# A first round over the key chunks with seven groups of queries, emitted with known landing times

## The chip, the cores and the metric

The kernel runs on one core of a Trainium2 chip. The metric is the device time of one execution in microseconds (us), and the median of several runs is quoted. The profile is that of one execution of the same program. PE is TensorE (PEld its weight loads), ACT is ScalarE, DVE is VectorE, POOL is GpSimd and SP is SyncE, which here only issues transfers.

## The reference

The reference is an attention with spatially reduced keys, followed by a two-layer feed-forward block over its output. Cut to what matters:

```python
B, C, H, W = 4, 128, 384, 32                 # N = H * W = 12288 queries of each b
kv_pool = kv.reshape(B, H // 4, 4, W // 4, 4, C).mean(axis=(2, 4))
k = v = kv_pool.reshape(B, -1, C) @ w_sr     # 768 keys of each b
s = (q @ k.transpose(0, 2, 1)) / np.sqrt(C)
a = np.exp(s - s.max(-1, keepdims=True))
a /= a.sum(-1, keepdims=True) + 1e-09
x = (a @ v).reshape(B * N, C)                # 49152 x 128
h = x @ w_in                                 # 128 x 2048
out = (h * (1.0 / (1.0 + np.exp(-1.702 * h)))) @ w_out
```

## The kernel before

**Tiling.** The 49152 queries form 96 groups of G = 512 (`NG`). The 768 keys of one batch element form JC = 6 chunks of 128. A unit of attention work is a pair (group i, chunk jc): one 128x512 score matmul (line 347), an exponential of its tile on ACT (line 349), and later the sums with the values, four 128-query tiles per group (line 360, four matmuls for each pair). A unit of feed-forward work is a pair (group g, chunk fc) with FCH = 16: one 128x512 matmul with `w_in` (line 593), the gelu on ACT (line 595), and one 128x512 matmul with `w_out` (line 603).

**Fills and drains.** The program is emitted in one fixed order. `seq` lists fills: one fill makes one to three units' matmuls into PSUM, then has ACT pass over all of them with one instruction into the buffer `ag`. Fill p uses banks 0 to 2 or 3 to 5 by the parity of p, so it waits until ACT has finished fill p-2. Fills are narrow at first: `sizes` gives two of one unit and then a number of two units, and after those all have three (K = 3); the last eight feed-forward fills have two units. Between two fills, drains are emitted: the matmuls that use what ACT has written (line 360 or 603). The loop at the end of the kernel decides how many drains fit, with a clock of its own in the emitting code: `now` is TensorE's position in units of one 512-column matmul, `end[p]` is when it thinks ACT will finish fill p, and `COST`, `COPY` and `free` hold the matmul times, the DVE copies, and when each accumulator bank becomes free. This clock decides the order of the instructions only; on the chip they wait on semaphores.

**Start.** POOL's queue issues the first loads in the order written in lines 245 to 257. A query group arrives from 256 KB of float32, a key chunk from 1 MB, both cast to bfloat16 by the transfer. Chunk 0 comes separately, through SP and a cast on the engines. For a chunk, `pool_chunk` (line 139: 16 small matmuls, then a DVE copy `pTc` at line 142) makes pooled columns; `key_and_value` (lines 161 and 162, copies at 163 and 164) makes keys `kT` and values `v`. For a query group, `transpose_q` (line 233, copy at line 239) makes `qT`. `first` says ahead of which fill each of these jobs stands. `warm(n)` puts n matmuls on ones (line 291), whose result nothing uses. The table `chunks` first runs over six groups for each chunk as it arrives, and then over the rest group by group.

**Later query groups.** Groups from 12 on come from `q_bf` with transposing transfers on SP (`load_qT`, line 215). Each is led by a one-column DVE memset (line 214) emitted when `TURN` reaches it. Line 412 is the score matmul of a pair whose exponential is computed on DVE (`early_fill`), emitted singly among the drains.

**End.** The last group (95) is drained by `drain_last` (line 631): 64 matmuls of 128 columns, spread over the four accumulator banks 2, 5, 6 and 7. One of these is still held by group 94 and is used from the tenth of these matmuls on. Group 94's result leaves its bank with a DVE transpose (line 614) after its last `w_out` matmul. Four copies (line 639) and two stores (line 642) end the program.

Of the kernel before, what the change touches and what calls it, by code (L numbers as in the profile page):

```python
# [24 lines left out]
def kernel(  # L25
# [8 lines left out]
    JC = J // 128  # L34
# [5 lines left out]
    NG = B * N // G  # L40
    NS = NG // 4
    GB = NG // B
# [38 lines left out]
    free = {2: 0.0, 5: 0.0, 6: 0.0, 7: 0.0}  # L81
    turns = [7, 6, 5]
    last_acc = 7
# [11 lines left out]
    def next_acc():  # L95
        return min((m for m in turns if m not in closes), key=lambda m: (max(free[m], now), turns.index(m)))
# [10 lines left out]
    now = 0.0  # L107
# [3 lines left out]
    def x_tile(s):  # L111
        return x[:, s % XS * SG:(s % XS + 1) * SG]
# [13 lines left out]
    def load_chunk(b, jc):  # L126

        a, ch = divmod(jc, HC)
        t = x_tile(XS - 1 - jc)
        nc.gpsimd.dma_start(out=t, in_=kv_r[b, a, ch])  # L130
        kv_tiles[b, jc] = t.rearrange("p (wp w1 c) -> p w1 wp c", w1=r, c=C)
# [75 lines left out]
    def cast_q(s):  # L207
        sl = slice(s * SG, (s + 1) * SG)
        nc.gpsimd.dma_start(out=q_bf[sl, :].rearrange("(p i) c -> p (i c)", p=128),
                            in_=q_flat[sl, :].rearrange("(p i) c -> p (i c)", p=128))  # L210
# [7 lines left out]
    QS = 3  # L218
    qs = [x_tile(XS - 1 - JC - s) for s in range(QS)]

    def load_q(s, lo, hi):
        nc.gpsimd.dma_start(  # L222
            out=qs[s].rearrange("p (g e) -> p g e", g=4)[:, lo:hi, :],
            in_=q_flat[s * SG + lo * G:s * SG + hi * G, :].rearrange("(g p i) c -> p g (i c)", p=128, i=4))
# [22 lines left out]
    load_chunk(0, 1)  # L247
    load_q(0, 2, 4)
    load_q(1, 0, 2)
    for jc in range(2, JC):  # L250
        load_chunk(0, jc)
    load_q(1, 2, 4)
    for s in range(2, QS):
        load_q(s, 0, 2)
        load_q(s, 2, 4)
    cast_q(3)
    cast_q(4)

# [68 lines left out]
    early = range(NG // R, NG // R + EARLY)  # L327
    rolling = [(i, JC - 1) for i in [*range(38, NG // R, 6), *range(57, 90, 6)]]
# [315 lines left out]


    NA, NM = NG * JC, NG * FCH
    chunks, sizes = [], [1] * 2 + [2] * 28
    chunks += [(0, 0), (1, 0), (0, 1), (1, 1)]
    chunks += [(i, jc) for i in range(2, 6) for jc in range(2)]
    chunks += [(i, jc) for jc in range(2, JC) for i in range(6)]  # L650
    chunks += [(i, jc) for i in range(6, NG) for jc in range(JC) if i not in early and (i, jc) not in rolling]
    seq, todo = [], []
    todo_early = [("a", t, a) for t in range(NT) for a in range(2) if (t // TS * TS + TS - 1) // 4 in early]
    for n in range(R):
        part = [c for c in chunks if c[0] // (NG // R) == n]
        while part:
            m = sizes.pop(0) if sizes else K
            seq.append(("a", part[:m]))
            part = part[m:]
# [34 lines left out]
    def later(g):  # L694
        extras.append((transpose_q, g))

    def jobs(p):

        nonlocal now
        for f, *args in first.get(p, ()):  # L700
            if f in COST:
                now = max(now, free[next_acc()])
            f(*args)
            if f in COST:
                now += COST[f][0]
                free[last_acc] = copied(f)

    def prepare(p):

        nonlocal now  # L710
        kind, part = seq[p]
        for i, jc in part:
            if (kind, i) not in begun:
                begun.add((kind, i))
                (background if kind == "a" else background_moe)(i)
            while kind == "a" and ((key_and_value, i // GB, jc) in extras or (transpose_q, i) in extras):
                f, *args = extras.pop(0)
                now = max(now, free[next_acc()]) + COST[f][0]
                f(*args)
                free[last_acc] = copied(f)  # L720

    first = {
        0: [(pool_chunk, 0, 0), (transpose_q, 0), (warm, 1), (key_chunk, 0, 0), (transpose_q, 1)],
        1: [(value_chunk, 0, 0), (warm, 1)],
        2: [(pool_chunk, 0, 1), (warm, 2), (key_and_value, 0, 1), (warm, 1), (transpose_q, 2)],
        3: [(transpose_q, 3)],
        4: [(transpose_q, 4)],
        5: [(transpose_q, 5)],
        6: [(pool_chunk, 0, 2)],
        7: [(key_and_value, 0, 2)],  # L730
        9: [(pool_chunk, 0, 3)],
        10: [(key_and_value, 0, 3)],
        12: [(pool_chunk, 0, 4)],
        13: [(key_and_value, 0, 4)],
        15: [(pool_chunk, 0, 5)],
        16: [(key_and_value, 0, 5), (later, 6)],
        17: [(later, 7)],
        18: [(later, g) for g in range(8, 12)]}

# [2 lines left out]
    COST = {pool_chunk: (1.9, 2.6), key_chunk: (0.3, 2.4), value_chunk: (0.3, 2.4),  # L744
            transpose_q: (1.05, 4.2), early_fill: (1.0, 5.5), key_and_value: (0.55, 3.5),
            transpose_pooled: (0.9, 3.6), make_k: (0.8, 3.2), make_v: (0.8, 3.7)}
# [8 lines left out]
    def on_dve(cost):  # L755
        nonlocal dve
        dve = max(dve, now + 1.0) + cost


    def copied(f):  # L760
        if f not in COPY:
            return now + COST[f][1]
        on_dve(COPY[f])
        return max(now + COST[f][1], dve)

    def fill(p):
        nonlocal now
        if p >= len(seq):
            return
        kind, part = seq[p]  # L770
        prepare(p)
        if p == 4:
            turns.insert(0, 2)
        if p == narrow - 5:
            for m in (2, 5):
                turns.remove(m)
        if p == narrow:
            assert not any(m in closes for m in (2, 5))
            now = max(now, free.pop(2), free.pop(5))
        lo = K * (p % 2)  # L780
        (fill_attn if kind == "a" else fill_moe)(part, banks[:, lo:lo + len(part), :])
        if p >= 2:
            now = max(now, end[p - 2] + HANDOVER / 2)
        now += len(part)
        begin = max(now + HANDOVER / 2, end[p - 1] if p else 0.0)
        if p and kind != seq[p - 1][0]:
            begin += SWITCH
        end.append(begin + FIXED + CHUNK * len(part))

    for p in range(2):  # L790
        jobs(p)
        fill(p)
    jobs(2)
    for n in range(len(seq)):
        fill(n + 2)
        jobs(n + 3)
        while True:
            room = room_ahead()
            limit = end[-1] - K - HANDOVER if n + 3 < len(seq) else 1e9
            bank = free[next_acc()]  # L800
            f = None
# [5 lines left out]
            if not f and not near and not steps and early_todo and early_fits(min(n + 2, len(seq) - 1), *early_todo[0]) and dve <= now + 2.0 and now >= bank:  # L807
                f, args = early_fill, early_todo[0]
            if f and max(now, bank) + COST[f][0] > limit + (0.0 if f is early_fill else 4.5) and room >= 4 * K:
                f = None  # L810
            if f:
                now = max(now, bank) + COST[f][0]
# [18 lines left out]
            kind, i, c = source[0]  # L831
# [18 lines left out]
            now = start + cost  # L850
# [39 lines left out]
```

The softmax here doesn't subtract the row's maximum and nothing guards it: scores larger than these inputs give would overflow.

## Time and profile before

| | before |
|---|---|
| median of 3 runs | 950.07 us |
| lowest, highest | 949.9, 951.19 us |
| span of the profiled execution | 948.6 us |
| busy: ACT | 934.9 us |
| busy: PE (ends modelled) | 941.8 us |
| busy: DVE | 536.5 us |
| granted TensorE clock | 1.0 |

Busy time is that in which an engine has an instruction running, and a PE that looks busy is not PE at its peak, since its matmuls are pipelined. A duration given for one instruction is longer than its share of the time where instructions overlap: for ACT's 128x1536 form the mean of one is 1507 ns, while starts in a steady row are some 1.336 us apart (13.16 us for 10 in the chain, with the page's rounding). The chain of waits is the list that is followed back from the last instruction; its shares tell what set the end.

### The profile page before, as it was taken

The page shows a single profiled execution, that of the slowest core. Times are in us where ns is not written, and L with a number is a line of the kernel's source. Part 1 is how long each engine was busy: PE and PEld are TensorE (multiplying, and loading weights), DVE is VectorE, ACT ScalarE, POOL GpSimd, SP SyncE. Part 2 cuts the span into 40 slices and gives each one's busy share as a digit, 9 for nine tenths or more (in the row PEclk, how much of TensorE's full clock was granted, in tenths as well). Part 3 has the DMA queues.
Part 4 walks back from the last instruction along what each step waited for, and adds up shares of the span by engine and source line. Part 5 has one row for each costly group of instructions (what it writes and reads, how often), then busy time and mean ns, then how long its engine had stood idle before and what let it go on. Part 6 is the DMA issues. An engine that isn't in the chain of part 4 may idle for free.

```text
span 948.6 us, 15423 instructions
## 1 busy us (share of the span) xinstructions
PE 941.8 (99%) x6314; PEld 502.9 (53%) x6314; DVE 536.5 (57%) x1035; ACT 934.9 (99%) x710; POOL 66.5 (7%) x114
## 2 busy tenths in 40 slices
PE   8999999999999999999999999999999999999998
PEld 4677776444444444454446777754444444444444
DVE  4643653102577777778655765365666665566631
ACT  6999999999999999999999999999999999999998
POOL 3101001320000232000000000000000000000000
PEclk9999999999999999999999999999999999999999
DMA  9999922999767799864335583562222222222222
GB/s 209 209 170 193 206 64 45 158 125 180 153 130 115 113 154 119 123 103 79 64 55 113 134 161 76 133 122 36 43 35 44 34 46 34 45 33 45 34 45 45
DMA packets 372855, 95.46 MB, mean 101 GB/s; under 512 B 346720, under 2 KB 370400, under 8 KB 372320
## 3 DMA queue, kind: packets, MB, share of 16 engines
q1 hardware_dynamic: 344000, 62.36, 36.9%
q0 software_dynamic: 28512, 31.99, 22.3%
q8 instruction: 49, 0.80, 0.4%
q14 instruction: 22, 0.18, 0.1%
q10 hardware_dynamic: 272, 0.13, 0.0%
HBM read 52.49 MB, written 48.76 MB: 107 GB/s over the span
## 4 chain that ended last, share of the span: by engine, by line
ACT 88%; PE 9%; DMA 2%; issue 0%; DVE 0%; POOL 0%; POOLq 0%
ACT ag L595 71%; ACT ag L349 17%; PE banks L347 4%; PE banks L360 3%; DMA qT<-q_bf 1%; DMA x<-in_kv_dram 1%; PE banks L139 0%; PE banks L593 0%; PE banks L631 0%; ACT L595 0%; PE banks L603 0%; PE banks L233 0%; ACT L349 0%; DVE kT L163 0%; POOL x L222 0%
## 5 line engine op out<-in xcount | busy, mean ns | idle before, releaser
L595 ACT ACTIVATE ag<-banks 128x1536 bf16<-128x1536 f32 (+1 forms) x510 | 682.2, 1507 | 0.0
L593 PE MATMUL banks<-x,w_in_sb 128*128 128x512 bf16 x1522 | 411.7, 379 | 0.1
L603 PE MATMUL banks<-ag,w_out_sb 128*128 128x512 bf16 x1506 | 407.8, 379 | 0.0
L349 ACT ACTIVATE ag<-banks 128x1536 bf16<-128x1536 f32 (+2 forms) x192 | 245.8, 1439 | 3.8 <-PE banks L347 3.4
L603 PEld LDWEIGHTS <-w_out_sb 128*128 128x128 bf16 x1520 | 148.4, 98 | 178.1 <-issue 0.9
L593 PEld LDWEIGHTS <-w_in_sb 128*128 128x128 bf16 x1522 | 147.3, 98 | 170.4 <-issue 1.1
L614 DVE STREAM_TRANSPOSE o_sb<-banks 128x512 f32<-128x512 f32 x95 | 67.9, 715 | 210.7 <-PE banks L603 195.0
L360 PEld LDWEIGHTS <-ag 128*128 128x128 bf16 x2272 | 146.1, 98 | 46.4 <-issue 0.6
L360 PE MATMUL banks<-v,ag 128*128 128x129 bf16 x2272 | 163.7, 220 | 0.1
L347 PE MATMUL banks<-qT,kT 128*128 128x512 bf16 x544 | 148.7, 379 | 1.6 <-DVE kT L163 1.0
L439 DVE SCALAR_TENSOR_TENSOR ea<-ea,eb 128x512 f32<-128x512 f32 x128 | 87.9, 687 | 3.2
L383 DVE RECIPROCAL rec<-banks 128x3 f32<-128x3 f32 x124 | 22.3, 180 | 95.9 <-PE banks L360 95.9
L386 DVE TENSOR_TENSOR x<-banks,rec 128x384 bf16<-128x384 f32 x124 | 69.1, 558 | 4.3
L347 PEld LDWEIGHTS <-kT 128*128 128x128 bf16 x544 | 46.3, 98 | 26.5 <-DVE kT L163 1.7
L470 DVE RECIPROCAL eb<-ea 128x256 f32<-128x256 f32 x28 | 47.6, 1727 | 0.5
L173 POOL DMA_DIRECT2D kvs<-in_kv_dram x32 | 40.4, 1299 | 17.8 <-DMA kvs<-in_kv_dram 15.2
L428 DVE TENSOR_SCALAR ea<-banks 128x512 f32<-128x512 f32 x32 | 22.1, 692 | 32.8 <-PE banks L412 32.5
L463 DVE SCALAR_TENSOR_TENSOR ea<-ea,eb 128x512 f32<-128x512 f32 x56 | 38.3, 685 | 1.6
L518 POOL MEMSET gate_tile<- 1x1 f32 x37 | 3.9, 105 | 326.6 <-DVE gate_tile L517 326.6
L434 DVE SCALAR_TENSOR_TENSOR eb<-eb,ea 128x512 f32<-128x512 f32 x32 | 22.1, 690 | 0.9
L450 DVE TENSOR_SCALAR qT<-banks 128x512 f32<-128x512 f32 x14 | 9.7, 692 | 17.2 <-PE banks L406 16.9
L441 DVE SCALAR_TENSOR_TENSOR ag<-ea,ee 128x512 bf16<-128x512 f32 x24 | 16.5, 688 | 0.7
(83 smaller groups left out, 267.9 us busy)
## 6 DMA issues: line engine op xcount, KB each, us to landing
out_dram<-o_sb SPq DMA_DIRECT2D x380, 64.0 KB, 2.0
kvs<-in_kv_dram POOLq DMA_DIRECT2D x32, 384.0 KB, 6.3
q_bf<-in_q_dram POOLq DMA_DIRECT2D x21, 512.0 KB, 6.9
x_bf<-x SPq DMA_DIRECT2D x13, 768.0 KB, 5.8
x<-in_kv_dram POOLq DMA_DIRECT2D x11, 512.0 KB, 10.4
x_bf<-x SPq DMA_DIRECT2D x6, 384.0 KB, 4.6
x<-in_q_dram POOLq DMA_DIRECT2D x5, 256.0 KB, 15.5
x<-in_kv_dram SPq DMA_DIRECT2D x1, 1024.0 KB, 5.1
```

The lines of the kernel that those rows point to most:

```text
L173: nc.gpsimd.dma_start(out=kv_sums[b][:, i2], in_=kv_p[b, i, w, :, i2], **({"accum_op": ADD} if n else {}))
L347: nc.tensor.matmul(ps[:, k, :], kTs[i // GB][:, jc * 128:(jc + 1) * 128], rhs, start=True, stop=True)
L349: nc.scalar.activation(place([("a",) + c for c in chunks]), ps, AF.Exp, scale=scale)
L360: nc.tensor.matmul(av_of[u][:, k * (C + 1):(k + 1) * (C + 1)], weights(("a", i, jc))[:, o:o + T], vs[i // GB][:, jc, 0:C + 1], start=(jc = ...
L386: nc.vector.tensor_tensor(to, ps[:, :, 0:C], rec.unsqueeze(2).broadcast_to([128, TS, C]), MUL)
L439: nc.vector.scalar_tensor_tensor(a, a, COEFFS[k], b, ADD, MUL)
L463: nc.vector.scalar_tensor_tensor(a, a, COEFFS[k], b, ADD, MUL)
L470: nc.vector.reciprocal(b[:, m:m + 256], a[:, m:m + 256])
L593: nc.tensor.matmul(ps[:, k, :], w_in_sb[:, fc * 128:(fc + 1) * 128], x[:, g % (4 * XS) * G:(g % (4 * XS) + 1) * G], start=True, stop=True)
L595: nc.scalar.activation(place([("m",) + c for c in chunks]), ps, AF.Gelu_apprx_sigmoid)
L603: nc.tensor.matmul(o_of[g], w_out_sb[:, fc, :], weights(("m", g, fc)), start=(fc == 0), stop=(fc == FCH - 1))
L614: nc.vector.transpose(o_sb, o_of.pop(g))
```

## The change

The first round takes seven query groups for each key chunk instead of six, so that one arriving chunk brings more work for ACT. For this, half of what was query load (1, 2:4) moves ahead of key chunk 2, and the transpose of group 6 stands ahead of fill 6 (fills are counted from 0). The jobs of the chunks and later groups shift by one to two fills. One `warm` matmul is dropped between the keys of chunk 1 and the transpose of group 2. One of the 28 two-unit fills is dropped from `sizes`.

The other part is in the emitting code: a table `LAND` gives times at which it takes the first loads to have landed, and `ready` holds when the copies behind a pooled chunk, a key chunk or a transposed query group are done. Its clock `now` is moved up to these times ahead of a job or a fill that uses them. This adds no wait on the chip; it changes how many drains the loop puts between fills.

```diff
+    load_q(1, 2, 3)
+    load_chunk(0, 2)
+    load_chunk(0, 3)
+    load_chunk(0, 4)
+    load_chunk(0, 5)
+    load_q(1, 3, 4)
+    load_q(2, 0, 2)
+    load_q(2, 2, 4)
-    for jc in range(2, JC):
-        load_chunk(0, jc)
-    load_q(1, 2, 4)
-    for s in range(2, QS):
-        load_q(s, 0, 2)
-        load_q(s, 2, 4)
...
-    chunks, sizes = [], [1] * 2 + [2] * 28
+    chunks, sizes = [], [1] * 2 + [2] * 27
     chunks += [(0, 0), (1, 0), (0, 1), (1, 1)]
-    chunks += [(i, jc) for i in range(2, 6) for jc in range(2)]
-    chunks += [(i, jc) for jc in range(2, JC) for i in range(6)]
-    chunks += [(i, jc) for i in range(6, NG) for jc in range(JC) if i not in early and (i, jc) not in rolling]
+    chunks += [(i, jc) for i in range(2, 7) for jc in range(2)]
+    chunks += [(i, jc) for jc in range(2, JC) for i in range(7)]
+    chunks += [(i, jc) for i in range(7, NG) for jc in range(JC) if i not in early and (i, jc) not in rolling]
...
+    def job(f, args):
...
+        now = max(now, free[next_acc()], LAND.get((f, *args), 0.0), ready.get((f, *args), 0.0))
+        f(*args)
+        now += COST[f][0]
+        free[last_acc] = copied(f)
+        if f is pool_chunk:
+            for then in (key_chunk, value_chunk, key_and_value):
+                ready[(then, *args)] = free[last_acc]
...
-        2: [(pool_chunk, 0, 1), (warm, 2), (key_and_value, 0, 1), (warm, 1), (transpose_q, 2)],
+        2: [(pool_chunk, 0, 1), (warm, 2), (key_and_value, 0, 1), (transpose_q, 2)],
...
-        6: [(pool_chunk, 0, 2)],
-        7: [(key_and_value, 0, 2)],
-        9: [(pool_chunk, 0, 3)],
-        10: [(key_and_value, 0, 3)],
+        6: [(transpose_q, 6)],
+        7: [(pool_chunk, 0, 2)],
+        8: [(key_and_value, 0, 2)],
+        10: [(pool_chunk, 0, 3)],
+        11: [(key_and_value, 0, 3)],
...
+    LAND = {(transpose_q, 0): 0.9, (transpose_q, 1): 3.8, (pool_chunk, 0, 1): 15.1, (transpose_q, 2): 21.0, (transpose_q, 3): 21.0, (transpose_q, 4): 26.9, (transpose_q, 5): 26.9, (transpose_q, 6): 29.8, (pool_chunk, 0, 2): 41.1, (pool_chunk, 0, 3): 52.5, (pool_chunk, 0, 4): 67.5, (pool_chunk, 0, 5): 78.8, (transpose_q, 7): 81.7, (transpose_q, 8): 87.6, (transpose_q, 9): 87.6, (transpose_q, 10): 93.5, (transpose_q, 11): 93.5}
...
+        if kind == "a":
+            now = max(now, *[ready.get(("k", i // GB, jc), 0.0) for i, jc in part], *[ready.get(("q", i), 0.0) for i, jc in part])
```

The order in which the two built programs hold their instructions differs in three respects that matter below. ACT's list is the same but for the place of one 128x1024 exponential, which moves from the narrow fills at the start to the end of the first attention half (27 and 1 instead of 28). TensorE's list has one matmul less (the `warm`), and many drains stand later: its first matmul of line 412 comes after 197 score matmuls and 582 drains, that of the old one after 196 and 600. The two ends are these (fill matmuls F, `w_out` matmuls D, and those of line 631 E; the last fills from left to right):

```
before: ... 2F 2D  2F 2D  2F 1D 3E  2F 9E  2F 52E
after:  ... 2F 2D  2F 2D  2F 2D     2F 2D  2F 2D 64E
```

More of the change, by code (lines that the diff above doesn't have):

```diff
@@ L695, in later @@
         extras.append((transpose_q, g))
+    def job(f, args):
+        nonlocal now
+        if f not in COST:
+            now += args[0] if f is warm else 0.0
+            f(*args)
+            return
+        now = max(now, free[next_acc()], LAND.get((f, *args), 0.0), ready.get((f, *args), 0.0))
+        f(*args)
+        now += COST[f][0]
[3 more added lines that the diff above has]
+                ready[(then, *args)] = free[last_acc]
+        if f in (key_chunk, key_and_value):
+            ready[("k", *args)] = free[last_acc] - (1.0 if f is key_and_value else 0.0)
+        if f is transpose_q:
+            ready["q", args[0]] = free[last_acc]
     def jobs(p):
-        nonlocal now
         for f, *args in first.get(p, ()):
[L701 to L706, printed above, removed]
+            job(f, args)
     def prepare(p):
@@ L717, in prepare @@
                 f, *args = extras.pop(0)
-                now = max(now, free[next_acc()]) + COST[f][0]
-                f(*args)
-                free[last_acc] = copied(f)
+                job(f, args)
     first = {
@@ L728 @@
         5: [(transpose_q, 5)],
-        6: [(pool_chunk, 0, 2)],
-        7: [(key_and_value, 0, 2)],
-        9: [(pool_chunk, 0, 3)],
-        10: [(key_and_value, 0, 3)],
[L733 to L738, printed above, removed]
+        6: [(transpose_q, 6)],
[3 more added lines that the diff above has]
+        11: [(key_and_value, 0, 3)],
+        14: [(pool_chunk, 0, 4)],
+        15: [(key_and_value, 0, 4)],
+        17: [(pool_chunk, 0, 5)],
+        18: [(key_and_value, 0, 5), (later, 7)],
+        19: [(later, 8)],
+        20: [(later, 9), (later, 10), (later, 11)]}
     FIXED, CHUNK, SWITCH, HANDOVER, EVACUATE = 0.295, 1.978, 6.0, 1.0, 4.5
@@ L764, in copied @@
         return max(now + COST[f][1], dve)
+    LAND = {(transpose_q, 0): 0.9, (transpose_q, 1): 3.8, (pool_chunk, 0, 1): 15.1, (transpose_q, 2): 21.0, (transpose_q, 3): 21.0, (transpose_q, 4): 26.9, (transpose_q, 5): 26.9, (transpose_q, 6): 29.8, (pool_chunk, 0, 2): 41.1, (pool_chunk, 0, 3): 52.5, (pool_chunk, 0, 4): 67.5, (pool_chunk, 0, 5): 78.8, (transpose_q, 7): 81.7, (transpose_q, 8): 87.6, (transpose_q, 9): 87.6, (transpose_q, 10): 93.5, (transpose_q, 11): 93.5}
+    ready = {}
     def fill(p):
```

## The prediction

> **What bounds the kernel now.** I read the page's busy times and chain first, then ACT's waits, then ACT's row in time, then the stages in which ACT is not busy throughout, then the end.
>
> ```profile
> span 948.6 us, 15423 instructions
> PE 941.8 (99%) x6314; PEld 502.9 (53%) x6314; DVE 536.5 (57%) x1035; ACT 934.9 (99%) x710; POOL 66.5 (7%) x114
> ACT 88%; PE 9%; DMA 2%; issue 0%; DVE 0%; POOL 0%; POOLq 0%
> ```
>
> ACT is busy for all but 13.7 us of the span, and 88% of the chain is ACT. Unless ACT's work changes, only those 13.7 us can be won. ACT's waits and its row show where they lie:
>
> ```profile
> ACT x L281 <- DMA x<-in_kv_dram: 3.9, 1, 3.9
> ACT ag L349 <- PE banks L347: 3.4, 3, 2.3
> ACT o_sb L639 <- DMA out_dram<-o_sb: 1.3, 1, 1.3
> ```
>
> ```profile
> 8.69 1.29 ACT L349 ACTIVATE ag<-banks 128x512 bf16<-128x512 f32 x2 [0.67 <-PE banks L347]
> 12.28 48.06 ACT L349 ACTIVATE ag<-banks 128x1024 bf16<-128x1024 f32 x44 [2.30 <-PE banks L347]
> ```
>
> The 3.9 us are the wait for chunk 0, and the 2.30 us ahead of 12.28 the wait for chunk 1. Behind 12.28 four stages (busy per engine, ACT's the fourth) hold nearly all the rest:
>
> ```profile
> 16.00:18.00 2.00, 1.61 (x22) 0.88 (x21) 0.49 (x2) 1.87 (x3) 0.43 (x1) 1.00 1.11 225
> 22.00:24.00 2.00, 1.80 (x27) 1.30 (x28) 0.90 (x3) 1.96 (x3) 0.00 (x0) 1.00 1.23 204
> 60.00:70.00 10.00, 10.00 (x142) 7.31 (x141) 4.67 (x19) 9.89 (x9) 0.00 (x0) 1.00 0.69 121
> 100.00:110.00 10.00, 9.88 (x113) 7.29 (x114) 8.10 (x19) 9.58 (x8) 0.00 (x0) 1.00 1.24 199
> ```
>
> That is 0.13 + 0.04 + 0.11 + 0.42 = 0.70 us. The last has its cause in the timeline: DVE reaches the memset that leads a query transfer only behind a drain's copy, the transfer lands late, and a line 412 matmul waits in TensorE's queue:
>
> ```profile
> 91.71 0.56 DVE L386 TENSOR_TENSOR x<-banks,rec 128x384 bf16<-128x384 f32 x1
> 92.22 0.06 DVE L214 MEMSET qT<- 128x1 bf16 x1
> ...
> 100.12 0.39 PE L412 MATMUL banks<-qT,kT 128*128 128x512 bf16 x1 [0.36 <-DMA qT<-q_bf]
> ```
>
> At the end ACT is no longer the bound: its row from 918.80 lasts 24.92 us, to 943.72, while TensorE still has 52 matmuls behind the last fill.
>
> ```profile
> 918.80 24.92 ACT L595 ACTIVATE ag<-banks 128x1536 bf16<-128x1536 f32 x21
> 940.53 0.38 PE L603 MATMUL banks<-ag,w_out_sb 128*128 128x512 bf16 x1
> 940.95 0.72 DVE L614 STREAM_TRANSPOSE o_sb<-banks 128x512 f32<-128x512 f32 x1 [6.45 <-PE banks L603]
> 941.95 0.59 PE L593 MATMUL banks<-x,w_in_sb 128*128 128x512 bf16 x2
> 942.38 3.07 PE L631 MATMUL banks<-w_out_sb,ag 128*128 128x128 bf16 x52
> 944.87 0.91 DVE L639 COPY o_sb<-banks 128x128 f32<-128x128 f32 x3 [3.21 <-PE banks L631]
> ```
>
> **What the Trainium skill says.** "PSUM — Partial Sum Buffer", section "Engine vs sequencer instructions", has the ACT, DVE and POOL queues as strict FIFO and TensorE's matmuls starting and completing in program order. The trace agrees where it matters: the memset above starts only as the copy ahead of it ends, and the 52 matmuls start 0.43 us behind the last fill's. "DMA: Bandwidth & Descriptors", section "Bandwidth", has 425 GB/s for a long transfer; the trace has the poolings of chunks 2 and 3, both waiting for data, at 14.89 and 17.50, so 1 MB in 2.61 us, 402 GB/s. I use the latter. "ScalarE: Activation LUTs", section "What ACT_TABLE_LOAD costs", prices an ACTIVATE by a constant and its columns; the trace has 1518 ns for 1536 columns and 1043 for 1024 (exponentials), again a constant and a part by columns.
>
> **The change part by part.**
>
> ACT's work: 0. Its list holds the same instructions of each form; one 128x1024 exponential only moves. So ACT's 934.9 us stay, and only idle time and the end can change.
>
> Start, chunk 1: -0.10. The loads up to chunk 1 keep their order, so its pooling starts at 9.85 as before. After it came keys (copy at 11.20, 0.29 long), the dropped warm matmul (11.10) and the transposes (11.42), then the score matmul at 11.65. Without the warm one the score matmul waits for the key copy: 11.49 plus 0.06 (the copy of chunk 2's keys ends at 16.44, its score matmul starts at 16.50), so 11.55. The 2.30 us are hardly touched.
>
> Chunk 2: 0, between -0.1 and +0.5. It lands later by 256 KB, a quarter of 2.61 = 0.65 us: 14.89 becomes 15.54. ACT gets one more narrow fill before it. 28 narrow exponentials took 26.2 us, 0.936 each; from 12.18 six of them last to 17.80 (before: five from 12.28, to 16.96). On TensorE pooling ends at 16.10, the fill of group 6 at 16.53, then the keys: matmul to copy 0.31, copy 0.29, to score matmul 0.06, so 17.2; score matmul to ACT is 0.64 (16.50 to 17.14 in the chain), so 17.85. ACT idles 0.05 instead of 0.13; if the chunk lands 0.2 later, 0.2. I take no difference.
>
> Later chunks: -0.04. Seven fills' halves per chunk are 7 x 0.468 = 3.28 us of ACT against 2.6 to 3.1 us between landings; six were 2.81, which starved ACT. The wait at 22 to 24 goes, and chunks 3 to 5 have a us of reserve.
>
> Drains of the middle: -0.11. Before, one interval in the stage at 60 to 70 has 15 drains and a pooling between two fills (about 1.3 us where ACT's 1.336 leave 0.69). In the new order poolings stand beside fewer drains, and no interval of this stage goes as high. Drains that stand later cost nothing there, since their results are wanted much later and the tiles have room.
>
> Query transfer: -0.42, between -0.42 and +0.4. The fills' boundaries shift by a unit, and the new order has the line 214 memset behind the copy of a drain that ends two score matmuls (0.9 us) earlier, with none directly ahead. Estimated, it starts at about 91.3 instead of 92.22. The chain gives 7.71 us from there to the landing at 100.07: now 99.1. TensorE reaches its line 412 matmul at 99.76 before; now it is one unit (0.445) later, six drains of 0.057 (0.34) earlier and some 0.2 earlier with everything: 99.7. It finds its data. If other transfers hold the landing at 100.07, the wait stays.
>
> End: +1.59, at least +1.10. The new order has 2 `w_out` matmuls and 64 of line 631 behind the last fill, where the old one had 52. Fills are paced by ACT in both, so the last one stays at 941.95 in this frame. Two `w_out` matmuls take 0.43; line 631 took 2.69 us for 48 in the chain, 0.056 each, so 12 more are 0.67: 1.10 in all. There is also a new wait. From the tenth matmul of line 631 on, the bank of group 94 is used, and its DVE transpose can start only after the last `w_out` matmul. That starts at 942.60; before, the transpose came 0.42 behind it (940.53 to 940.95) and took 0.72, so the bank is free at 943.74, and TensorE goes on at 943.80. It has done nine by 942.81 + 0.50 = 943.31: 0.49 lost, with 55 matmuls queued behind the wait, and copies and stores behind those. Before, the transpose was through at 941.67 and hidden beside a fill. Nothing stands behind the end to hide it.
>
> Sum: -0.10 - 0.04 - 0.11 - 0.42 + 1.59 = +0.92 us; 950.07 becomes 951.0.
>
> **The rivals.** *Starved at chunk 2, transfer not helped:* chunk 2's landing shifts more than its bytes do (+0.5), the line 412 matmul waits 0.4 longer, and the end costs 1.59: with nothing won elsewhere +2.5, 952.6. For it: poolings already wait for transfers; against it: the trace's steady rate. *End absorbed:* the longer tail is hidden in some way, and the idle time is won: -0.67, 949.4. For it: the last 16 matmuls have ACT's last result to wait for; against it: in the chain the end is matmuls without a wait, the last of ACT being done at 943.72. *The start pays:* the 2.30 us before 12.28 mostly go, with the 0.67, against 1.10 at the end: -1.9, 948.2. Against it: chunk 1 arrives no earlier.
>
> **How the numbers follow.** The forecast has 0.66, starvation 0.17, the absorbed end 0.12, the paying start 0.05. The time is 951.0. From 949.3 to 952.5 the range takes in both bounds of the forecast's terms and the absorbed end. Faster by over 0.2% is below 948.17: only the paying start, 0.05. Slower is above 951.97: most of the starvation and a sliver of the forecast, 0.16. The rest, 0.79, is within 0.2%.
>
> **What would show it.** Right: ACT's sum near 934.9; its row starting at 12.1 to 12.2; no wait before line 412 near 100; behind the last fill two `w_out` matmuls, nine of line 631, then a gap of half a us ended by the transpose of line 614; ACT's last gelu some 0.7 us earlier but the span longer. Wrong: an ACT gap of over 0.3 us at 17 to 18, a late landing at line 412, or a tail without that gap. If ACT shows new waits elsewhere, I misjudged the drains.

## The result, and the profile after

| | before | after |
|---|---|---|
| median of 6 runs | 950.28 us (949.9 to 951.6) | 953.44 us (953.2 to 953.7) |
| ratio to before | | 1.0031, 95% interval 1.0018 to 1.0044 |
| span of the profiled execution | 948.6 us | 951.7 us |
| end of ACT's last gelu | 943.72 us | 945.24 us |
| from there to the end of the span | 4.88 us | 6.46 us |

The change costs 3.2 us. Half lies ahead of ACT's last gelu (945.24 - 943.72 = 1.52) and half behind it (6.46 - 4.88 = 1.58). The head of the page and the chain of the changed kernel:

```profile
span 951.7 us, 15427 instructions
PE 942.7 (99%) x6313; PEld 503.0 (53%) x6313; DVE 536.2 (56%) x1035; ACT 935.1 (98%) x710; POOL 66.3 (7%) x115
PE 96%; DMA 2%; ACT 2%; DVE 0%; POOL 0%; issue 0%; POOLq 0%
```

ACT's work is the same (935.1 against 934.9), but the chain that was 88% ACT is now 96% PE: followed back from the new tail, it stays on TensorE, which hands over from fill to drain with hardly a pause. Both engines are near their limit, so a small change turns the chain over (it is 66% PE in e3 below and 56% ACT in e4, two variants of this change); its shares alone don't say which is worth more. ACT's waits, and the four stages shown of before:

```profile
ACT ag L351 <- PE banks L349: 4.9, 3, 2.2
ACT x L283 <- DMA x<-in_kv_dram: 3.9, 1, 3.9
ACT o_sb L641 <- DMA out_dram<-o_sb: 2.9, 1, 2.9
```

```profile
16.00:18.00 2.00, 1.49 (x13) 0.65 (x10) 0.79 (x4) 2.00 (x4) 0.39 (x2) 1.00 1.09 221
22.00:24.00 2.00, 1.78 (x27) 1.14 (x25) 0.87 (x4) 2.00 (x3) 0.00 (x0) 1.00 1.16 194
60.00:70.00 10.00, 9.78 (x141) 7.14 (x140) 4.83 (x18) 9.91 (x9) 0.00 (x0) 1.00 0.54 116
100.00:110.00 10.00, 8.53 (x98) 6.30 (x99) 6.40 (x16) 8.03 (x7) 0.00 (x0) 1.00 1.06 235
```

The seven-group round does what it is for: ACT (the fourth of the busy times) no longer idles at 16 to 18 and 22 to 24, 0.17 us won. At 100 to 110 it idles 1.97 us, where it idled 0.42. The timeline there:

```profile
90.88 0.56 DVE L388 TENSOR_TENSOR x<-banks,rec 128x384 bf16<-128x384 f32 x1
91.39 0.06 DVE L214 MEMSET qT<- 128x1 bf16 x1
...
101.47 0.39 PE L414 MATMUL banks<-qT,kT 128*128 128x512 bf16 x1 [1.89 <-DMA qT<-q_bf]
```

The memset that leads the query transfer comes 0.83 us earlier than before (91.39 against 92.22), and yet TensorE waits 1.89 us for the transfer instead of 0.36 (line 414 is line 412 of before; lines from 256 on have moved). The end:

```profile
943.46 0.59 PE L595 MATMUL banks<-x,w_in_sb 128*128 128x512 bf16 x2
943.89 0.59 PE L605 MATMUL banks<-ag,w_out_sb 128*128 128x512 bf16 x2
944.33 0.67 PE L633 MATMUL banks<-w_out_sb,ag 128*128 128x128 bf16 x9
944.52 0.72 DVE L616 STREAM_TRANSPOSE o_sb<-banks 128x512 f32<-128x512 f32 x1 [6.68 <-PE banks L605]
945.30 3.23 PE L633 MATMUL banks<-w_out_sb,ag 128*128 128x128 bf16 x55 [0.31 <-DVE o_sb L616]
```

Two `w_out` matmuls and nine of the last drain follow the last fill, then TensorE waits for the DVE transpose, and 55 matmuls stand behind that wait.

### The profile page after: what moved, and what is told of

Read it like the earlier page. It is cut to its first block, busy times and chain, and to the rows that moved or that the text cites. A ratio compares the mean times of both kernels' runs of the same rounds, so it can differ in the third digit from the quotient of the medians.

```text
span 951.7 us, 15427 instructions
## 1 busy us (share of the span) xinstructions
PE 942.7 (99%) x6313; PEld 503.0 (53%) x6313; DVE 536.2 (56%) x1035; ACT 935.1 (98%) x710; POOL 66.3 (7%) x115
## 4 chain that ended last, share of the span: by engine, by line
PE 96%; DMA 2%; ACT 2%; DVE 0%; POOL 0%; issue 0%; POOLq 0%
PE banks L595 35%; PE banks L605 35%; PE banks L362 13%; PE banks L349 11%; ACT ag L351 2%; DMA qT<-q_bf 1%; DMA x<-in_kv_dram 1%; PE banks L414 1%; PE banks L139 0%; PE banks L408 0%; PE banks L633 0%; PE banks L233 0%; POOL x L222 0%; DVE o_sb L616 0%; PE banks L184 0%
```

## The experiments

Two questions were open: why a transfer that starts earlier lands later, and whether the longer tail is really the price of the drains left out at the start. The first theory on the transfer was that it shares the DMA engines with the `w_out` load, which POOL issues some us before. Labels name the kernel that was edited (before or after). Ratios are to the kernel before, run beside them, whose medians were 950.31 (e1 to e4), 950.46 (e5 to e8) and 950.38 (e9 to e12).

**e1 and e2: the `w_out` load out of the way.** The same edit in both kernels:

```diff
-        if i == 28:
+        if i == 32:
             gate()
             nc.gpsimd.dma_start(out=w_out_sb, in_=moe_w_out.rearrange("(o p) c -> p o c", p=128))
```

> The changed kernel with the w_out load (and its gate) issued at group 32 instead of 28; all else as it is, the end of the program too. Theory 1 (the query transfer of group 36 to 39 is slow because it shares the DMA engines with the w_out load of small packets): it lands some 5 us after its issue, the line 412 matmul finds its data, ACT is idle for under 0.1 us at 95 to 105 instead of 1.97, and the time falls by about 1.9 us, from 953.4 to 951.5. Rival (the transfer is slow by itself or by the bring-back transfer behind it on the same queue): it still takes 9 to 10 us, and the time stays at 953.4. In both the tail behind the last gelu stays at about 6.4 us.

> The kernel before with the same edit. Theory 1: the wait of 0.36 us at line 412 and ACT's idle 0.42 us at 100 to 110 go; the time falls from 950.3 to 949.9. Rival: no change.

Measured: the changed kernel falls to 951.28 us (1.0009, 1.0001 to 1.0018), the kernel before to 949.86 (0.9994, 0.9985 to 1.0002). In both, line 412 finds its data and ACT is busy throughout 90 to 110. The transfer, issued at 91.35, lands after 6.3 us instead of 9.9, and the matmul of the changed kernel starts without a wait:

```profile
99.28 0.38 PE L414 MATMUL banks<-qT,kT 128*128 128x512 bf16 x1
```

The tail of the changed kernel stays at 6.46. So the two losses are separate. Without the wait its last gelu ends at 943.04, 0.68 us ahead of that of before and 0.40 ahead of that of e2, which has the same edit. Of the 1.42 us between e1 and e2 the tail makes 1.6; as an estimate from these two, the new round wins some 0.2 us at the start.

**e3 and e4: each half of the change alone.** In e3 the tables are emptied; in e4 the kernel before gets them (landing times of chunks 2 to 5 lowered by 2.9 units, that of query group 6 set to 78.8, where its load now stands).

```diff
 e3, on after
-    LAND = {(transpose_q, 0): 0.9, ...
+    LAND = {}
...
-            ready["q", args[0]] = free[last_acc]
 e4, on before
+        now = max(now, free[next_acc()], LAND.get((f, *args), 0.0), ready.get((f, *args), 0.0))
+    LAND = {..., (pool_chunk, 0, 2): 38.2, (pool_chunk, 0, 3): 49.6, ...
```

> The changed kernel without LAND and ready: seven groups, new load order, one warm matmul less, but the emitting clock as before. Built, its line 412 matmul stands behind 588 drains (600 before, 582 changed), its w_out gate on DVE behind the same drain unit as in the changed kernel, and its end is 1 w_out matmul and 64 of line 631 behind the last fill. If the late w_out load makes the wait, it is here too: 1.5 to 2.5 us at line 412, tail 6.2 us, time about 953. Rival (the emitting clock causes the loss): 950.3 and a wait under 0.5.

> The kernel before with LAND and ready (landing times moved back by the 256 KB for chunks 2 to 5), six groups and the old load order. Built, 582 drains before the line 412 matmul, w_out gate one score matmul earlier than in the changed kernel, end as in the seven-group one. If drains that stand later cost at the end and shift the gates, the tail is 6.2 us, a wait of 1 to 2 us at line 412, time 952 to 953. Rival (seven groups cause the loss): 950.3.

Measured: seven groups alone 951.39 us (1.0011, 1.0004 to 1.0018), with a wait of 0.74 at line 412 and a tail of 6.16; the emitting clock alone 952.42 (1.0021, 1.0013 to 1.0029), wait 1.04, tail 6.18. Neither rival holds: each half brings a longer tail and a longer wait by itself. But neither makes the transfer late by itself: it lands at 99.7 in e3 and at 100.1 in e4, against 100.1 before. Their waits grow because TensorE comes to the matmul 0.78 and 0.66 us earlier, with fewer drains ahead of it (588 and 582 for 600). The late landing comes only with both halves together. My numbers for e3, time and wait, were too high.

**e5: the load earlier.** With `i == 27` in place of 28.

> The changed kernel with the w_out load and its gate moved the other way, from group 28 to 27 (right behind the w_in load). If the loss comes from the w_out load reaching into the query transfer, and the size goes with the landing of w_out, w_out lands 2 to 4 us earlier and the wait at line 412 shrinks from 1.89 us to under 0.5: about 951.5. Rival (only the absence of the load near the transfer helps): wait stays above 1.5, 953.4.

Measured: 953.46 us (1.0032, 1.0021 to 1.0043), wait 2.45. The theory's form was wrong: `w_out` was issued at 84.13 instead of 87.77 and landed at 101.0 instead of 100.7. Something ahead of it in POOL's queue sets when its data move. POOL's row shows what; first of before, then of after:

```profile
78.09 0.09 POOL L518 MEMSET gate_tile<- 1x1 f32 x1 [25.23 <-DVE gate_tile L517]
78.32 0.96 POOL L209 DMA_DIRECT2D q_bf<-in_q_dram  x2
```

```profile
79.57 0.09 POOL L520 MEMSET gate_tile<- 1x1 f32 x1 [26.97 <-DVE gate_tile L519]
79.80 0.96 POOL L209 DMA_DIRECT2D q_bf<-in_q_dram  x2
```

Two casts of query groups, two more, `w_in` and `w_out` follow one another, and from the first cast's packets (79.5 before, 81.0 after) to the last of `w_out`'s the queue has hardly a pause. The packets of 256 bytes that are `w_out`'s begin at 92.98 before and at 93.83 after. The first cast waits for a gate, a memset on DVE that in the changed kernel's order stands behind another drain's copy: 79.57 instead of 78.09.

**e9 and e10: the row of casts moved.**

```diff
 e9, on after
-    CAST = {0: [5], 13: [6], 14: [7], 15: [8], 25: [9, 10], 26: [11, 12]}
+    CAST = {0: [5], 13: [6], 14: [7], 15: [8], 24: [9, 10], 26: [11, 12]}
 e10, on before
+    CAST = {0: [5], 13: [6], 14: [7], 15: [8], 26: [9, 10, 11, 12]}
```

> The changed kernel with the casts of query groups 36 to 43 (two transfers, and their gate) issued at group 24 instead of 25; w_in and w_out as in the changed kernel. Theory (one POOL queue works through casts, w_in and w_out in order without a pause, so the late gate of the casts is what delays w_out's small packets, not w_out's own gate): the first packets of w_out come 1.5 us or more earlier than 94.0, they end before 98, and the wait at line 412 falls from 1.89 us to under 0.6: about 951.5. Rival (w_out's own gate matters): w_out is issued at the same 87.8, the wait stays above 1.5, 953.4.

> The kernel before with all four of those casts at group 26. Theory: the queue's row of casts, w_in and w_out starts some 2 to 3 us later, the wait at line 412 grows from 0.36 us to between 1.5 and 3, and the kernel before loses 1 to 2.5 us, 951.3 to 952.8, with its tail of 4.9 us unchanged. Rival: no change.

Measured: e9 951.89 us (1.0019, 1.0010 to 1.0029), wait 0.50 with `w_out` issued at 87.69 as in the changed kernel; e10 956.78 (1.0067, 1.0052 to 1.0082), tail 4.87 as before, and the wait is

```profile
104.78 0.61 PE L412 MATMUL banks<-qT,kT 128*128 128x512 bf16 x1 [4.74 <-DMA qT<-q_bf]
```

The direction is confirmed on both kernels. The size in e10 was well above what I gave: 6.4 us lost where I gave 1 to 2.5, a wait of 4.74 where I gave 1.5 to 3. There the transfer and `w_out` run side by side for over 6 us. ACT's idle time at 100 to 110 is 6.03 us, more than the wait, and TensorE's granted clock has a part in it, which I hadn't reckoned with: it is 1.00 until 104, 0.50 from 105 to 107, and 1.00 again from 108. The first three score matmuls behind the wait take 1.48 us, where three take 0.81 else. After the waits of 1.89 us in the changed kernel and 2.45 in e5 the clock stayed at 1.00.

In all nine runs of the table below `w_out`'s packets begin 14.0 to 15.9 us after the first cast, whether `w_out` itself is issued at 84.13 (e5) or at 87.77. So it is the row of casts that sets when they move.

**e11: the transfer later.**

```diff
-    TURN = {6: 3, 7: 4, 8: 5, 20: 6, 21: 7, 22: 8, 30: 9, 32: 10, 35: 11, 40: 12}
+    TURN = {6: 3, 7: 4, 8: 5, 20: 6, 21: 7, 22: 8, 31: 9, 32: 10, 35: 11, 40: 12}
```

> The changed kernel with the query transfer for groups 36 to 39 issued at group 31 instead of 30, some 2.5 to 3 us later. Theory (what sets its landing is the end of w_out's packets, which it shares the engines with): it lands within 1 us of 101.4 all the same, wait 1 to 3 us, 952.5 to 954.5. Rival (the landing follows the issue): 104, a wait of 4.5 us, 956.

Measured: 952.77 us (1.0024, 1.0015 to 1.0034), below the changed kernel's 953.44.

```profile
100.82 0.39 PE L414 MATMUL banks<-qT,kT 128*128 128x512 bf16 x1 [1.31 <-DMA qT<-q_bf]
```

The transfer was issued 3.90 us later (95.43 instead of 91.53), landed 0.65 earlier (100.77 instead of 101.42), and the wait fell to 1.31. `w_out`, issued at the same time, landed 2.3 us earlier (98.4 instead of 100.7). So an early start of the transfer takes from both. The queues of the changed kernel at 96 to 98 (packets, MB, share of 16 engines):

```profile
q0 software_dynamic: 664, 0.17, 82.9%
q1 hardware_dynamic: 663, 0.17, 64.2%
```

q0 carries `w_out`, q1 the transfer: 664 and 663 packets, and in e10 from 97 to 103 they are 1815 and 1821. The Trainium skill, "DMA: Bandwidth & Descriptors", section "Queues, rings and completion order", says that each engine takes turns between the queues it has work for, a packet at a time. The equal counts agree with equal turns; the page's packet holds several descriptors, and whether it is what the trace counts isn't shown. While both queues have work on all engines, each gets some 330 packets of 256 bytes per us; `w_out` alone gets about 680 (e11, 95 to 96: 683) and transposing transfers alone about 1130 (after, from 101). The counts aren't equal throughout: in the kernel before, from 95.84 to 98.20, where `w_out` runs out, they are 479 and 946. In the table, `w_out`'s landing is its issue plus its time to landing, and the transfer's is the start of the line 412 matmul that waited for it:

| | first cast | transfer issued | `w_out` landed | transfer landed | TensorE there | wait |
|---|---|---|---|---|---|---|
| before | 78.32 | 92.36 | 98.5 | 100.1 | 99.76 | 0.36 |
| after | 79.80 | 91.53 | 100.7 | 101.4 | 99.58 | 1.89 |
| e3 | 78.87 | 92.25 | 98.0 | 99.7 | 98.98 | 0.74 |
| e4 | 77.66 | 91.05 | 98.8 | 100.1 | 99.10 | 1.04 |
| e5 | 79.55 | 91.27 | 101.0 | 101.8 | 99.32 | 2.45 |
| e6 (below) | 79.45 | 92.83 | 98.8 | 100.4 | 99.39 | 1.01 |
| e9 | 76.39 | 91.44 | 98.6 | 100.0 | 99.50 | 0.50 |
| e10 | 82.58 | 92.63 | 105.1 | 104.8 | 100.04 | 4.74 |
| e11 | 79.73 | 95.43 | 98.4 | 100.8 | 99.51 | 1.31 |

The transfer lands between 0.3 us ahead of `w_out` and 2.4 us behind it, but 5.3 to 12.1 us behind its own issue: its landing goes with that of `w_out`.

**e6, e7, e8 and e12: the drains back to the start.**

```diff
-            limit = end[-1] - K - HANDOVER if n + 3 < len(seq) else 1e9
+            limit = end[-1] - K - HANDOVER + (0.6 if n < 110 else 0.0) if n + 3 < len(seq) else 1e9
```

e6 is this edit on the changed kernel; e7, e8 and e12 have `w_out` at group 32 as well, with 0.6, 1.0 and 0.8 (e7 and e8 also ask there that drains are left; e6 and e7 have the same 603 drains ahead of line 412).

> The changed kernel with the loop's limit raised by 0.6 units for its first 110 steps; built, 603 drains instead of 582 stand before the line 412 matmul, and the end has again 1 w_out matmul, 3, 9 and 52 matmuls of line 631 around and behind the last fills, as before. If the drains left out at the start are what is paid at the end, and TensorE has idle time for them at the start, the tail behind the last gelu falls from 6.46 to 4.9 us and the time by 1.6 us plus or minus the wait at line 412, whose transfer is not touched: 951.3 to 952.3. Rival (TensorE is full at the start): ACT idles about 1.2 us more in the first 100 us and the time stays near 953.4.

> Both edits on the changed kernel: w_out at group 32 and the limit raised by 0.6. If the two losses are separate, 951.28 less 1.58 for the tail: 949.7, ACT's last gelu at 943.0 and a tail of 4.9 us. Rival (TensorE full at the start): 950.9.

> As the run with both edits, with the limit raised by 1.0: 627 drains before the line 412 matmul, and only 32 matmuls of line 631 behind the last fill. If early drains are still free, the tail loses up to 20 matmuls of 0.056 us more, held by ACT's last gelu: tail about 4.4 us, time 949.2. If TensorE is full by now, ACT idles 1 us or more in the first 100 us and the time is 950 or above.

> The changed kernel with w_out at group 32 and the limit raised by 0.8: 618 drains before the line 412 matmul, 32 matmuls of line 631 behind the last fill. If TensorE still has room at the start: 949.0 to 949.5. If it is full, as with 1.0, ACT falls behind by 1 us or more and the time is 950 to 951.5.

Measured: e6 950.77 us (1.0001, 0.9992 to 1.0009), tail 4.83, wait 1.01; e7 949.53 (0.9988, 0.9982 to 0.9995), tail 4.85, no wait; e12 949.88 (0.9994, 0.9986 to 1.0003), tail 4.2; e8 952.2 (1.0017, 1.0011 to 1.0024), tail 4.1. Twenty-one drains more before line 412 (603 for 582) give the whole tail back, and ACT does not pay for them: its last gelu ends at 942.85 in e7 and at 943.04 in e1. In e6 the wait shrank too, since its memsets shifted again, so e6 is below what I expected. e7 is 0.9 us faster than the kernel before, of which the later `w_out` gave 0.45 in e2 without the change; its end is that of before:

```profile
941.51 3.07 PE L633 MATMUL banks<-w_out_sb,ag 128*128 128x128 bf16 x52
```

With 45 drains more (e8) TensorE is over-full: ACT now waits for fills, and its last gelu ends at 946.39 instead of 942.85 in e7, far more than the tail wins. The gaps are the smaller part of these 3.5 us; ACT's busy time itself is 936.9 us against 934.7. In e12, with 36 more, the last gelu comes 1.0 us later than in e7, nearly all of it busy time (935.7). There ACT's passes from 60 to 141 us start 1.346 us apart in the median, in e7 1.330. That they follow late fills is likely, but wasn't tried apart. Three of the gaps of e8, in ACT's row:

```profile
63.84 2.89 ACT L351 ACTIVATE ag<-banks 128x1536 bf16<-128x1536 f32 x2 [0.25 <-PE banks L349]
67.04 2.89 ACT L351 ACTIVATE ag<-banks 128x1536 bf16<-128x1536 f32 x2 [0.31 <-PE banks L349]
70.25 11.19 ACT L351 ACTIVATE ag<-banks 128x1536 bf16<-128x1536 f32 x8 [0.32 <-PE banks L349]
```

## Why the prediction was wrong

I gave 951.0 us and a range up to 952.5; it was 953.44. Term by term:

- ACT's work, 0: right, 0.2 us of difference.
- Start, chunk 1, -0.10: the mechanism was right. From pooling (9.91) to the score matmul (11.61) it is 1.70 us as worked out, against 1.80 before. But chunk 1 landed 0.06 later, and 12.26 against 12.28 is what is left.
- Chunk 2, 0, and later chunks, -0.04: measured -0.13 and -0.04. The round of seven feeds ACT without a gap. One reading was off: of the two poolings that give 2.61 us for 1 MB, the second's weight load starts at 17.33, ahead of its matmul at 17.50, so 2.44 us. The pooling of chunk 2 came 0.70 us later (15.59 for 14.89), close to the 0.65 worked out.
- Drains of the middle, -0.11: measured -0.02. The stage at 60 to 70 idles 0.09 us still. That drains moved back cost nothing *there* held; they cost at the end, where I counted them.
- **Query transfer, -0.42, between -0.42 and +0.4: the step that failed.** Measured +1.55 (1.97 against 0.42 us of ACT's idle time). The memset was right (91.39 for 91.3), and so was TensorE's arrival (99.58 for 99.7). What failed is taking the 7.71 us from issue (92.36) to landing as the transfer's own and carrying it over. Of these us most were spent beside the `w_out` load. With the first cast 1.48 us later, the packets of `w_out` came 0.85 us later, and the transfer was issued 0.83 earlier: the two ran side by side for 3.9 us (95.56 to 99.48) instead of 2.4 (95.84 to 98.20), and the transfer took 9.89. e1, e9, e10 and e11 show it. The prediction did say that other transfers might hold the landing at 100.07, which would leave the wait as it was, and gave +0.4 as the upper bound without a working. How much later the landing could come wasn't worked out, nor what else would be in the queues.
- End, +1.59: measured 1.58, with the wait for the group-94 transpose as worked out (the tenth matmul starts at 945.30, 0.97 us after the first, against 0.50 for nine). e6 and e7 show that it is the drains left out at the start that are paid here.

The sum of what was measured is -0.02 - 0.13 - 0.04 - 0.02 + 1.55 + 1.58 = 2.9, plus 0.2 of ACT's busy time, of the 3.1 us between the two spans. The rival that came nearest had the transfer's wait in it, but with the wrong reason, a late chunk 2.

What stays open: how the 1.35 us by which the transfer landed later divide between the late casts and its own early start, since they act on each other (e9 moves the one, e11 the other, and each helps only in part). And in the changed kernel the two queues move almost nothing for about a us near 99.5 (28 packets from 99.25 to 100.0), with the transfer unfinished; a packet of the instruction queue, from 98.38 to 99.38, lies just ahead of it. e5, e9 and e11 have stretches of 0.5 to 0.75 us with hardly more (29 packets from 97.0 to 97.75 in e5), so it doesn't set the changed kernel apart. What causes them wasn't tried. Each variant has one profile, so a few tenths of a us between two of them may be chance.

## What to carry to other kernels

A time from issue to landing belongs to the queues as they were when it was measured. Before it is carried over to another moment, see what else is in flight then, and how many packets it has; beside a load of small packets an early issue can bring a later landing. A change to an emission order can move every small instruction that gates a transfer, so it is the gates' places behind other work, not the edited lines alone, that are to be followed. And where two engines are both nearly full, work that one leaves undone at the start stays in its backlog to the end: count it there.

## What the runs showed of the hardware

- Two queues with 256-byte packets got equal packet counts while both had work (664 and 663 in 2 us, 1815 and 1821 in 6 us of e10), and together no more than one of them reached alone: some 660 per us against 680 for the `w_out` load and 1130 for transposing transfers.
- Issuing the transposing transfer 3.90 us later brought it in 0.65 us earlier and the load beside it 2.3 us earlier (e11).
- Moving the casts so that the first starts 4.3 us later made the kernel before 6.4 us slower (e10), through one matmul that waits 4.74 us in TensorE's queue, and through the granted clock behind it, which was 0.50 from 105 to 107. Waits of 1.89 and 2.45 us left it at 1.00.
- In e12 ACT was busy 1.0 us longer than in e7 for the same 710 instructions, with hardly more idle time, and its last gelu came 1.0 us later: the gaps in its row don't show all that it lost.
